# Agent attention and maxout FFN: queries turned on TensorE, keys still turned by DMA

## The chip, the core and the metric

The kernel runs on one core of a Trainium2 chip. The metric is the device time of one execution in microseconds; the median of three runs is taken. The engines named below are TensorE (PE for its matmuls, PEld for its weight loads), VectorE (DVE), ScalarE (ACT), GpSimd (POOL) and SyncE (SP), which here only issues DMAs.

## What is computed

```python
B, N, C = (4, 12544, 128); n_agents = 49; d_ff = 768
def _attn_ref(q, k, v, agents):
    scale = 1.0 / np.sqrt(q.shape[-1])
    def sm(a, b):                       # softmax over the last axis
        s = scale * (a @ b.transpose(0, 2, 1))
        s = s - s.max(-1, keepdims=True)
        e = np.exp(s)
        return e / (e.sum(-1, keepdims=True) + 1e-09)
    agent_v = sm(agents, k) @ v
    return sm(q, agents) @ agent_v
def _moe_ref(x, w1, w2, w3, w_out):     # x: the attention's rows
    h = np.maximum(np.maximum(x @ w1, x @ w2), x @ w3)
    return h @ w_out
```

The 49 agents first read all 12,544 keys and values of a batch; then every query attends to the 49 agents, and each resulting row passes the FFN. Inputs and output are float32; the kernel works in bfloat16.

## The kernel before

A batch has 98 tiles of 128 rows, taken in 13 groups: twelve of 8 tiles (1,024 rows) and a last one of 2. There are 52 key groups (`k_group`) and 52 query groups (`q_group`). A key group is loaded, cast to bf16 on POOL, turned by a DMA transpose on SP (line 159), multiplied with the agents (`scores`, line 166), put through exp on ACT, and multiplied with the values and with ones (`values`, lines 178 and 180); DVE adds the sums into `Eacc` (`accumulate`, line 189). After a batch's last key group `k_tail` folds agent values and FFN weights into one matrix `G` (line 220). A query group is loaded, cast on POOL (line 249), turned by a DMA transpose on SP (line 253), multiplied with the agents (`scores`, line 259), put through exp (line 264), and multiplied with slices of `G`.

The maxout is written with two relus. For each of six slices f of the hidden width, `first(f)` on TensorE fills a `uv` tile, `relu_first(f)` on ACT takes its relu to `a_sb` (line 301), `second(f)` fills another `uv` tile, and `max_second(f)` on DVE takes the maximum into `r` (line 312). For f = 5 both steps are relus on ACT (lines 298 and 310) and `first(5)` and `second(5)` share one tile. Each `first` or `second` is two matmuls of line 287, on two halves of the rows. `out_linear` (line 317) and `out_hidden` (line 326) sum the result in an `o` tile, and `out_scale` on DVE (line 333) divides by the sum of the exponentials, which `recips` prepared from `sums` (line 273).

[...] three `uv` tiles of two banks, one `o` tile and one `m` tile. The single `m` buffer is handed from user to user: key scores with values and query sums, then query scores, then key scores again. An operation that takes a new `m` tile waits until the readers of the old one are done.

The order of all work is written out by hand. Each step is entered with a key, a float that counts slots; the steps are sorted by it, equal keys in the order of entry, and each engine executes its own in that order. Query group i has `key` 6i, so one group takes six slots. The key group one batch and one group ahead has the same key. In the six slots of a period TensorE's order is therefore, by key within the period: `out_linear(0)` 0.1, `out_hidden` 0.3, key `scores` 0.65, `second(1)` 1.0, `first(2)` 1.05, `out_hidden` 1.3, `second(2)` 2.0, `sums` and `first(3)` 2.05, `out_hidden` and key `values` 2.3, `second(3)` 3.0, `first(4)` 3.05, `second(4)` 4.0, `first(5)` 4.05, `out_linear(1)` 4.06, query `scores` of the next group 4.25, `out_hidden` 4.3, `second(5)` 5.0, `first(0)` of the next group 5.05, `out_hidden` 5.3, then `second(0)` and `first(1)` of the next group. DVE's order is `out_scale(1)` 0.1, three `max_second`, `recips` 2.6, `accumulate` 2.75, `out_scale(0)` 2.9, and two more `max_second` at 3.5 and 4.5.

Of the kernel before, what the change touches and what calls it, by code (L numbers as in the profile page):

```python
# [10 lines left out]
BF16 = mybir.dt.bfloat16  # L11
# [5 lines left out]
def kernel(  # L17
# [18 lines left out]
    nc = tc.nc  # L36
# [4 lines left out]
    P = 128  # L41
    NF = Dff // P
    H = 64
    GT = 8
# [10 lines left out]
    work = ctx.enter_context(tc.tile_pool(name="work", bufs=2))  # L55
# [8 lines left out]
    def m_tile(dtype=FP32):  # L64
        return psum.tile([P, 512 if dtype == FP32 else 1024], dtype, tag="m", bufs=1, name="m_ps")
# [3 lines left out]
    def at(key, fn):  # L69
        ops.append((key, len(ops), fn))  # L70


    ident = const.tile([P, P], BF16, name="ident")
# [3 lines left out]
    agT = const.tile([P, B, H], BF16, name="agT")  # L77
# [9 lines left out]
    for i, w in enumerate((moe_w1, moe_w2, moe_w3)):  # L87
        t = const.tile([P, Dff], FP32, name=f"wst{i}")
# [143 lines left out]
    def q_group(b, g):  # L232
        n, t0 = sizes[g], starts[g] * P
        nh = n // 2
        T = nh * P
        pairs = [range(0, min(2, nh)), range(2, nh)]
        key = 6.0 * (NG * b + g)
        d = {}
# [10 lines left out]
            nc.gpsimd.tensor_copy(out=d["qb"][:, :n, :], in_=d["q"][:, :n, :])  # L249

        def transposes():
            d["qT"] = work.tile([P, GT, P], BF16, tag="qT", bufs=3, name="qT")
            nc.sync.dma_start_transpose(out=d["qT"][:, :n, :],
                                        in_=d["qb"][:, :n, :].rearrange("p j c -> p (j c)"))

        def scores():
            t = d["s"] = m_tile()
            for h in range(2):
                nc.tensor.matmul(t[h * H:(h + 1) * H, :T], agT[:, b, :], d["qT"][:, h:n:2, :],  # L259
                                 start=True, stop=True, skip_group_check=True)  # L260

        def exps():
# [79 lines left out]

        at(key - 24, load)
        at(key - 14, cast)
        at(key - 10.2, transposes)
        at(key - 1.75, scores)
        at(key - 1.3, exps)
        at(key + 2.05, sums)
# [21 lines left out]
    for b in range(B):  # L370
        for g in range(NG):
            k_group(b, g)
            q_group(b, g)
# [34 lines left out]
```

## Time and profile before

| | |
|---|---|
| median of 3 runs | 603.34 us (602.93 to 603.52) |
| profiled execution | 602.93 us, its span 601.1 us |
| loads and stores on SP | 512 KB each; 48 of each of k, v, q and out, and 4 small ones of each |
| DMA transposes on SP | 52 of kT, median 5.2 us to landing; 52 of qT, median 4.5 us |
| HBM traffic | 78.74 MB read, 25.69 MB written |

The span runs from the first to the last instruction of the profiled execution. A line of the groups gives busy time, the mean duration of one, and the idle time of the engine just before, with what ended it. Three stages are to be kept apart. Until about 70 us only key groups of the first batch run. From there to about 450 us query groups of one batch and key groups of the next run together. After that only queries of the last batch are left.

### The profile page before, as it was taken

What the parts mean: (1) busy time and instruction counts of PE and PEld (TensorE: products, weight loads), DVE (VectorE), ACT (ScalarE), POOL (GpSimd) and SP (SyncE); (2) the same over time, 40 slices, a digit from 0 to 9 for tenths busy, and PEclk for the clock granted to TensorE, in tenths of its full rate; (3) what the DMA queues carried; (4) which work ended last, traced back from release to release, by engine and by line L of the source; (5) the groups of instructions that cost most, each with busy time, mean ns of one, the idle gap of its engine ahead of it and who ended that gap; (6) DMA issues with size and microseconds to landing.
All of it is one profiled execution on the core that took longest, in us unless ns stands there. A gap on an engine that the chain in (4) does not pass through costs nothing.

```text
span 601.1 us, 13157 instructions
## 1 busy us (share of the span) xinstructions
PE 471.4 (78%) x5320; PEld 285.2 (47%) x5320; DVE 383.8 (64%) x499; ACT 412.5 (69%) x493; POOL 140.3 (23%) x149
## 2 busy tenths in 40 slices
PE   0343588898987889888887878889896898889886
PEld 0333245555553545555553545555553444545454
DVE  1200267878786556878776568787875667766774
ACT  2542378787875667787875678878784577777773
POOL 1223543233142232323142232322000101010000
PEclk9999999999998969999997989999996889988999
DMA  8999999999898797989986899995732625533222
GB/s 325 370 340 343 341 275 303 270 294 219 252 239 225 222 277 198 270 269 202 255 261 196 216 284 224 284 257 159 181 110 53 189 77 147 145 119 101 67 75 81
DMA packets 135112, 130.99 MB, mean 218 GB/s; under 512 B 107079, under 2 KB 110091, under 8 KB 135051
## 3 DMA queue, kind: packets, MB, share of 16 engines
q1 hardware_dynamic: 133632, 128.48, 76.7%
q10 hardware_dynamic: 1419, 1.67, 0.8%
q8 instruction: 41, 0.67, 0.5%
q14 instruction: 20, 0.16, 0.1%
HBM read 78.74 MB, written 25.69 MB: 174 GB/s over the span
## 4 chain that ended last, share of the span: by engine, by line
PE 49%; ACT 18%; DVE 15%; DMA 9%; issue 6%; SPq 1%; POOL 1%; ACTq 0%; POOLq 0%; DVEq 0%
PE uv_ps L287 20%; PE o_ps L326 18%; ACT a_sb L301 14%; DVE r L312 12%; DMA kT<-k_bf 6%; PE o_ps L317 4%; PE m_ps L259 3%; DVE o_sb L333 3%; ACT r L310 2%; DMA qT<-q_bf 1%; PE m_ps L178 1%; PE m_ps L180 1%; DMA wst<-in_moe_w_dram 1%; PE m_ps L220 1%; POOL k_bf L150 1%
## 5 line engine op out<-in xcount | busy, mean ns | idle before, releaser
L312 DVE TENSOR_TENSOR r<-uv_ps,a_sb 128x1024 bf16<-128x1024 f32 (+1 forms) x260 | 295.0, 1158 | 40.7 <-ACT a_sb L301 27.7
L301 ACT ACTIVATE a_sb<-uv_ps 128x1024 bf16<-128x1024 f32 (+1 forms) x260 | 248.3, 975 | 71.7 <-PE uv_ps L287 69.9
L287 PE MATMUL uv_ps<-e_q,G 49*128 49x512 bf16 (+1 forms) x1248 | 211.8, 391 | 55.0 <-ACT a_sb L301 43.6
L326 PE MATMUL o_ps<-wo_bf,r 128*128 128x128 bf16 x2352 | 184.1, 227 | 0.0
L326 PEld LDWEIGHTS <-r 128*128 128x128 bf16 x2352 | 144.4, 101 | 52.0 <-issue 49.2
L287 PEld LDWEIGHTS <-G 49*128 49x128 bf16 x1248 | 65.5, 95 | 131.8 <-issue 93.4
L333 DVE TENSOR_TENSOR o_sb<-o_ps,recips 128x512 f32<-128x512 f32 (+1 forms) x100 | 67.0, 670 | 95.1 <-PE o_ps L326 95.1
L249 POOL CAST q_bf<-q_st 128x1024 bf16<-128x1024 f32 (+1 forms) x52 | 51.7, 994 | 154.3 <-DMA qT<-q_bf 150.0
L155 POOL CAST v_bf<-v_st 128x1024 bf16<-128x1024 f32 (+1 forms) x39 | 38.7, 993 | 207.4 <-PE m_ps L180 187.2
L298 ACT ACTIVATE uv_ps<-uv_ps 128x1024 f32<-128x1024 f32 (+1 forms) x52 | 49.9, 959 | 28.5 <-DVE r L312 16.0
L310 ACT ACTIVATE r<-uv_ps 128x1024 bf16<-128x1024 f32 (+1 forms) x52 | 50.7, 975 | 21.5 <-PE uv_ps L287 21.4
L150 POOL CAST k_bf<-k_st 128x1024 bf16<-128x1024 f32 (+1 forms) x52 | 51.9, 998 | 55.5 <-DMA kT<-k_bf 46.4
L317 PE MATMUL o_ps<-G,e_q 128*128 128x256 bf16 x196 | 40.3, 287 | 12.7 <-DVE o_sb L333 12.5
L166 PE MATMUL m_ps<-agT,kT 128*128 128x49 bf16 x392 | 20.9, 196 | 25.7 <-DMA kT<-k_bf 24.4
L178 PE MATMUL m_ps<-e_k,v_bf 128*128 128x49 bf16 x392 | 30.8, 195 | 8.7 <-ACT e_k L171 8.7
L171 ACT ACTIVATE e_k<-m_ps 128x392 bf16<-128x392 f32 (+1 forms) x52 | 25.0, 480 | 16.1 <-PE m_ps L166 15.8
L189 DVE TENSOR_TENSOR Eacc<-m_ps,Eacc 128x98 f32<-128x98 f32 x48 | 10.6, 221 | 35.7 <-PE m_ps L180 35.7
L264 ACT ACTIVATE e_q<-m_ps 128x512 bf16<-128x512 f32 (+1 forms) x52 | 29.5, 568 | 3.7 <-PE m_ps L259 3.6
L317 PEld LDWEIGHTS <-e_q 128*128 128x128 bf16 x196 | 15.0, 98 | 35.1 <-issue 34.5
L180 PE MATMUL m_ps<-e_k,ones 128*128 128x49 bf16 x392 | 30.9, 194 | 0.0
L180 PEld LDWEIGHTS <-ones 128*128 128x128 bf16 x392 | 26.0, 103 | 10.0 <-issue 10.0
L166 PEld LDWEIGHTS <-kT 128*128 128x128 bf16 x392 | 17.3, 104 | 28.3 <-DMA kT<-k_bf 25.7
(43 smaller groups left out, 137.3 us busy)
## 6 DMA issues: line engine op xcount, KB each, us to landing
k_st<-in_k_dram SPq DMA_DIRECT2D x48, 512.0 KB, 5.4
v_st<-in_v_dram SPq DMA_DIRECT2D x48, 512.0 KB, 6.2
q_st<-in_q_dram SPq DMA_DIRECT2D x48, 512.0 KB, 4.2
out_dram<-o_sb SPq DMA_DIRECT2D x48, 512.0 KB, 2.9
wst<-in_moe_w_dram ACTq DMA_DIRECT2D x3, 384.0 KB, 7.8
kT<-k_bf SPq DMA_TRANSPOSE x52, 5.2
qT<-q_bf SPq DMA_TRANSPOSE x52, 4.5
k_st<-in_k_dram SPq DMA_DIRECT2D x4, 128.0 KB, 4.6
```

The costliest lines, as they stand in the source:

```text
L150: nc.gpsimd.tensor_copy(out=d["kb"][:, :n, :], in_=d["k"][:, :n, :])
L155: nc.gpsimd.tensor_copy(out=d["vb"][:, :n, :], in_=d["v"][:, :n, :])
L180: nc.tensor.matmul(t[:, c + A:c + 2 * A], ones, e, start=False, stop=True, skip_group_check=True)
L249: nc.gpsimd.tensor_copy(out=d["qb"][:, :n, :], in_=d["q"][:, :n, :])
L287: nc.tensor.matmul(t[:, h, :T], G[b][h * H:h * H + A, col + f * P:col + (f + 1) * P], d["e"][h * H:h * H + A, :T], start=start, stop=True, ...
L298: nc.scalar.activation(u, u, AF.Relu)
L301: nc.scalar.activation(a_sb[f][:, :, :T], u, AF.Relu)
L310: nc.scalar.activation(r[:, :, :T], u, AF.Relu)
L312: nc.vector.tensor_tensor(out=r[:, :, :T], in0=u, in1=a_sb[f][:, :, :T], op=ALU.max)
L317: nc.tensor.matmul(t[:, i * 2 * C:(i + 1) * 2 * C], d["e"][:, jj * P:(jj + 1) * P], G[b][:, C1O:C1O + 2 * C], start=(i == 0), stop=False, ...
L326: nc.tensor.matmul(t[:, c:c + C], r_sb[f][:, h, jj * P:(jj + 1) * P], wo_bf[:, f, :], start=False, stop=(f == NF - 1), skip_group_check=True)
L333: nc.vector.tensor_tensor(out=d["out"][:, j:j + m, :], in0=d["o", o][:, :m * C].rearrange("p (j c) -> p j c", c=C), in1=d["r"][:, j:j + m] ...
```

## The change

Only the query side changes. The DMA transpose of line 253 goes. In its place the eight 128x128 blocks of a group are turned by eight TensorE transposes (matmuls against an identity) into an `m` tile of bf16, and a new step `evacuate` copies that tile on DVE to `qT` in SBUF. The blocks of even and odd tiles are put apart on the way, so that `scores` reads two contiguous halves. The transposes are entered at key - 3.0 (before: key - 10.2) and the copy at key - 2.6. `qT` has two buffers in place of three. The keys' side keeps its DMA transposes.

```diff
         def transposes():
-            d["qT"] = work.tile([P, GT, P], BF16, tag="qT", bufs=3, name="qT")
-            nc.sync.dma_start_transpose(out=d["qT"][:, :n, :],
-                                        in_=d["qb"][:, :n, :].rearrange("p j c -> p (j c)"))
+            t = d["qT_ps"] = m_tile(BF16)
+            for j in range(n):
+                jj, h = divmod(j, 2)
+                i = h * nh + jj
+                nc.tensor.transpose(t[:, i * P:(i + 1) * P], d["qb"][:, j, :], ident)
+
+        def evacuate():
+            d["qT"] = work.tile([P, GT * P], BF16, tag="qT", name="qT")
+            nc.vector.tensor_copy(out=d["qT"][:, :n * P], in_=d["qT_ps"][:, :n * P])
 
         def scores():
             t = d["s"] = m_tile()
             for h in range(2):
-                nc.tensor.matmul(t[h * H:(h + 1) * H, :T], agT[:, b, :], d["qT"][:, h:n:2, :],
+                nc.tensor.matmul(t[h * H:(h + 1) * H, :T], agT[:, b, :], d["qT"][:, h * T:(h + 1) * T],
                                  start=True, stop=True, skip_group_check=True)
...
-        at(key - 10.2, transposes)
+        at(key - 3.0, transposes)
+        at(key - 2.6, evacuate)
```

## Prediction

> **What bounds the kernel now.** First the page. TensorE is the busiest engine, but no engine is full, and its clock is mostly, not always, granted.
>
> ```profile
> span 601.1 us, 13157 instructions
> PE 471.4 (78%) x5320; PEld 285.2 (47%) x5320; DVE 383.8 (64%) x499; ACT 412.5 (69%) x493; POOL 140.3 (23%) x149
> PEclk9999999999998969999997989999996889988999
> ```
>
> Next the list of waits from 76 us to the end, TensorE alone. Its first two lines:
>
> ```profile
> PE uv_ps L287 <- ACT a_sb L301: 43.6, 52, 0.9
> PE o_ps L317 <- DVE o_sb L333: 12.5, 47, 0.8
> ```
>
> No line of that list names a DMA. Over the whole span the page has 24.4 us of TensorE waiting for kT, all in the first 76 us, where keys run alone; TensorE waited 0.9 us for qT, once.
>
> Then the chain of waits in a stretch of steady state, one period of 9.73 us (relu to relu, 128.47 to 138.21):
>
> ```profile
> 135.00 1.24 DVE r L312
> 136.23 0.04 issue
> 136.27 0.39 PE uv_ps L287 x2
> 136.67 0.55 PE o_ps L326 x8
> ...
> 137.57 0.03 PE m_ps L178
> 137.60 0.03 PE m_ps L180
> 137.63 0.56 PE uv_ps L287 x4
> 138.18 0.02 issue
> 138.21 1.03 ACT a_sb L301
> 139.24 0.04 issue
> 139.28 0.39 PE uv_ps L287 x2
> ```
>
> The period is a closed loop: `max_second(1)`, `first(3)`, `out_hidden`, the key values, `second(3)` and `first(4)` (the x4), `relu_first(4)` on ACT, `first(5)`, and by way of TensorE, ACT and DVE back. There is no slack on it. What is put between the values and `first(4)` lengthens every period.
>
> The timeline of the same place, by engine, shows what lies beside it:
>
> ```profile
> 137.67 0.21 DVE L279 RECIPROCAL recips<-m_ps 128x8 f32<-128x8 f32 x1 [0.25 <-PE m_ps L180]
> 137.79 0.21 DVE L189 TENSOR_TENSOR Eacc<-m_ps,Eacc 128x98 f32<-128x98 f32 x1
> 137.92 0.68 DVE L333 TENSOR_TENSOR o_sb<-o_ps,recips 128x512 f32<-128x512 f32 x1
> 138.52 2.35 DVE L312 TENSOR_TENSOR r<-uv_ps,a_sb 128x1024 bf16<-128x1024 f32 x2
> 142.53 0.69 DVE L333 TENSOR_TENSOR o_sb<-o_ps,recips 128x512 f32<-128x512 f32 x1 [1.67 <-PE o_ps L326]
> ```
>
> The `m` tile is free of its readers only when `accumulate` ends, at 138.00.
>
> **What the Trainium skill says.** "TensorE: Matmul & The Clock Gate", Part 4, says that a TensorE transpose goes to PSUM and needs a copy after it, and that in transpose mode it "doesn't count as PE-busy the same way". On the time this trace disagrees with nothing: the six transposes of the weights (line 123) lasted 314 ns at the median and started within 0.5 us (24.5 to 25.0), as did six plain matmuls of the same shape (line 127, 26.0 to 26.5). On the counting no run here shows anything. Part 1 of that page says that the clock is halved or given back by the activity of windows of about 3.4 us; the trace agrees, and shows how near the edge this kernel runs (below). "VectorE: DVE Perf Modes", tier table, allows a copy out of PSUM at most twice the base rate. "Perfetto Trace Analysis", Matmuls, advises rotating PSUM banks so that evacuation overlaps; here the transposes have the one `m` bank.
>
> **The change part by part.** *Removed:* 52 DMA transposes and their issues on SP. As no wait of TensorE after 76 us names a DMA, and the first qT is issued at 61.99 us, behind the chain's last kT (53.41), I count this at nothing. POOL's 150.0 us of waiting for qT turn into waits of the same cast for the transposes of two groups before, as `qb` has two buffers. Those end at that group's key - 3, one slot before the cast at key - 14 of the later group is due. The casts of k and v and then SP's kT, queued behind it, have 14 slots, some 23 us, until the key scores; kT lands in 5.2 us. That is the cover; without it a late kT would stop TensorE.
>
> *Eight transposes, in TensorE's order.* Their key ties with `second(3)`, which was entered earlier; so they stand after `second(3)` and before `first(4)`. They wait for `accumulate`: 138.00 + 0.05 = 138.05. Eight 128x128 matmuls cost 0.55 us in the chain until the next thing starts, changeover included. `first(4)` started at 137.79 (timeline); now 138.60: **+0.81 us**, 0.26 of waiting and 0.55 of work. Waiting behind them are `first(4)`, and through it ACT's relu, `first(5)` and the rest of the loop.
>
> *The copy on DVE.* Nearest row: w1T, 768 bf16 out of PSUM, 557 ns; four copies of 49 took 179 ns. So 0.53 ns an element, 1,024 take 0.69 us. It runs from about 138.7 to 139.4, between `out_scale(0)` and `max_second(3)`, which start 0.8 late. Who needs them: the query scores, before at 139.93, now 140.74, need the copy (1.3 us to spare); `first(0)`, about 141.3 before and 142.1 now, needs the tile of `max_second(3)`, which ends about 140.6. So it costs nothing. Its upper bound, at the base rate, is near the 1.2 us of a 1,024-wide row of line 312: still within the 1.3. DVE's idle 1.67 us before `out_scale(1)` takes it up.
>
> *The groups.* In batches 0 to 2 the 33 full groups g = 1 to 11: 33 x 0.81 = 26.7. Their three groups of two tiles, work 0.21 in place of 0.55: 3 x 0.47 = 1.4. The first groups of batches 1 to 3 stand behind `k_tail`, whose last copy ended at 191.42 in the first case, and run at half clock, where twelve of line 326 took 1.46 us: about 3 x 1.1 = 3.3. Batch 3 has no `accumulate`: the transposes wait for `recips` (end 576.28), 576.33 + 0.55 = 576.88 in place of `first(4)` at 576.22, 0.66 each: 11 x 0.66 + 0.3 = 7.6. The very first group: `Eacc`'s copy ends at 69.54, transposes at half clock and their latency 1.1, copy 0.7; scores at 71.4 in place of 70.12: 1.3. Two more groups at the cold start pay 0.4 extra each: 0.8. Sum **41.1 us**; 602.93 + 41.1 = 644.0 for the profiled execution, and 644 against the median 603.34, 0.4 us above it.
>
> **The rivals.**
>
> *The clock falls.* The windows view, over stretches that end where the clock record changed or could have:
>
> ```profile
> 524.40:527.80 3.40, 2.46 (x25) 1.20 (x24) 3.34 (x5) 2.60 (x3) 1.04 (x1) 1.00 0.93 248
> 527.80:531.20 3.40, 3.40 (x20) 1.67 (x21) 1.34 (x2) 1.61 (x2) 0.00 (x0) 0.50 0.00 0
> 575.60:579.00 3.40, 2.48 (x23) 1.01 (x21) 3.40 (x5) 2.61 (x3) 0.00 (x0) 1.00 0.01 2
> 128.40:131.80 3.40, 2.50 (x26) 1.19 (x21) 2.73 (x3) 2.54 (x3) 1.60 (x3) 1.00 1.22 196
> ```
>
> After the first comes half clock, after the third and fourth not: the lowest windows are already at the edge, 2.46 of 3.40 us busy against 2.48. The change puts a wait into just that part of the period, where `first(5)` already waits 0.90 us. If the transposes count as work, I take the windows to stay about where they are. If not, the low window loses 0.45 us more. Each halving in batch 3 made its two exp-to-exp intervals together 1.4 us longer (9.79 + 10.52 against 2 x 9.43). A low stretch of about 1.9 us, met by windows 3.4 us apart, is hit in 0.56 of the periods: 48 x 0.56 x 1.4 = 38 us on top, **682**. For it: the skill's sentence. Against it: a transpose moves as many columns at the same pace.
>
> *The transposes are slower than matmuls when the clock is full.* The trace has them only in the cold start, 107 ns apart. If they kept to that pace, 8 x 0.05 more per group, 20 us in all: **664**.
>
> *VectorE becomes the bound.* Should the copy or `max_second(3)` miss its margin of 1.3 us, its 0.69 enters the loop as well: 48 x 0.69 = 33, **677**. Against it: DVE has 23% idle in a period.
>
> *The other side.* The loop has 0.90 us of idle TensorE before `first(5)` in every period. If the transposes ran there, 0.55 would vanish in it, and as work they would lift the low windows and save the two halvings in batch 3, 2.8 us: **600.5**. It decides where `first(4)` is delayed by less than about 0.1 us. Against it: the order of equal keys.
>
> **How the numbers follow.** The sum holds: 0.50. The clock falls: 0.36. VectorE: 0.06. Slow transposes: 0.04. The other side: 0.04. The likeliest is 644, its own range 634 to 655 (0.26 of waiting and changeover either way, 48 times 0.2). The range goes to 702, to take in most of the clock's case, 660 to 720. Faster by over 0.2%, about what a measurement of this kernel can tell from no change: 0.03; within it 0.02; slower 0.95.
>
> **What would show it.** Right: the exp of the queries comes every 10.55 us in place of 9.73 in steady state, `first(4)` starts some 0.6 us after `accumulate` ends, PE waits a little for `Eacc`, and the copies last about 0.69 us. The clock's case: half clock in many slices of the steady state. Wrong: an interval under 9.9, `first(5)`'s wait shrunk, or TensorE waiting for kT.

## The result, and the profile after

| | before | after |
|---|---|---|
| median, and its runs | 603.43 us (602.93 to 606.06, 4 runs) | 645.76 us (645.34 to 646.15, 4 runs) |
| profiled execution, span | 602.93 us, 601.1 us | 645.34 us, 643.6 us |

The ratio is 1.0692, 95% interval 1.066 to 1.0724. The change is slower, by 42.5 us between the two spans. The forecast was 644. Here and below a median is that of all runs, while a ratio leaves out runs more than 1.5% above the fastest of their kernel.

The lines of the changed kernel have moved: transposes 256, copy 260, query scores 265, query exp 270, `recips` 285, `first` and `second` 293, `relu_first` 307 (304 for f = 5), `max_second` 318 (316), `out_linear` 323, `out_hidden` 332, `out_scale` 339. The key side has its old lines. First the page after: totals, clock, and the two new groups (line, operation, count | busy, mean ns | idle before it, and what ended most of that).

```profile
PE 506.0 (79%) x5712; PEld 309.5 (48%) x5712; DVE 417.2 (65%) x551; ACT 412.1 (64%) x493; POOL 138.3 (21%) x149
PEclk9999999999998979999996779999997959999999
...
L260 DVE COPY qT<-m_ps 128x1024 bf16<-128x1024 bf16 (+1 forms) x52 | 34.3, 660 | 12.4 <-PE m_ps L256 11.1
L256 PE MATMUL m_ps<-ident,q_bf 128*128 128x128 bf16 x392 | 32.2, 227 | 8.9 <-DVE Eacc L189 6.0
```

The shares are nearly those of before, and the clock has its dips only at the batch changes. The two dips that batch 3 had before are gone. So 42.5 us went without an engine becoming busier in its share: a sign of a longer loop, not of a fuller engine. The waits of TensorE from 80 us on say the same (us in total, times, longest):

```profile
PE uv_ps L293 <- ACT a_sb L307: 43.9, 52, 0.9
PE o_ps L323 <- DVE o_sb L339: 12.5, 47, 0.8
PE m_ps L256 <- DVE Eacc L189: 6.0, 31, 0.2
```

The first two are the old ones, unchanged (43.6 and 12.5 before). The third is the new one. TensorE waits as long for ACT as before, and does 0.5 us more ahead of it. The chain of waits in one period (start, length, what):

```profile
145.03 0.39 PE uv_ps L293 x2
145.42 0.55 PE o_ps L332 x8
...
146.42 0.21 DVE recips L285
146.62 0.14 DVE Eacc L189
146.76 0.14 issue
146.90 0.61 PE m_ps L256 x8
147.50 0.34 PE uv_ps L293 x2
...
147.87 1.03 ACT a_sb L307
148.90 0.04 issue
148.94 0.39 PE uv_ps L293 x2
```

Where `second(3)` and `first(4)` stood together in one x4 before, the chain now leaves TensorE for `recips` and `accumulate` on DVE, comes back with 0.14 us of "issue", spends 0.6 on the transposes, and only then reaches `first(4)` (the x2 at 147.50), ACT's relu and `first(5)` (148.94). The timelines of TensorE and DVE there show where the loop was cut open, and what lies beside it:

```profile
146.90 0.61 PE L256 MATMUL m_ps<-ident,q_bf 128*128 128x128 bf16 x8 [0.19 <-DVE Eacc L189]
147.44 0.61 PE L293 MATMUL uv_ps<-e_q,G 49*128 49x512 bf16 x4
148.94 0.39 PE L293 MATMUL uv_ps<-e_q,G 49*128 49x512 bf16 x2 [0.90 <-ACT a_sb L307]
...
149.59 0.41 PE L265 MATMUL m_ps<-qT,agT 128*64 128x512 bf16 x2
```

```profile
146.54 0.21 DVE L189 TENSOR_TENSOR Eacc<-m_ps,Eacc 128x98 f32<-128x98 f32 x1
146.67 0.68 DVE L339 TENSOR_TENSOR o_sb<-o_ps,recips 128x512 f32<-128x512 f32 x1
147.54 0.69 DVE L260 COPY qT<-m_ps 128x1024 bf16<-128x1024 bf16 x1 [0.19 <-PE m_ps L256]
```

The 0.68 of `out_scale` lies beside the wait and the transposes. TensorE idles before the transposes and again, 0.90 us, before `first(5)`. The copy ends at 147.54 + 0.69 = 148.23, and the query scores that need it start at 149.59, 1.36 later. In the whole span they waited for it 0.8 us in total.

Starts of the query exps in the two traces, from one group to the next, give the loss by place:

| | before, us | after, us | difference | in the forecast's sum |
|---|---|---|---|---|
| first exp | 70.80 | 72.36 | +1.56 | +1.3 |
| batch 0, first and second interval | 9.95, 11.26 | 11.21, 13.54 | +1.26, +2.28 | +1.2 each |
| steady interval, batches 0 to 2 | 9.73 | 10.65 | +0.92 | +0.81 |
| steady interval, batch 3 | 9.43 | 10.08 | +0.65 | +0.66 |
| batch 0 (first exp to that of batch 1) | 132.3 | 145.4 | +13.1 | +11.3 |
| batch 1 | 135.5 | 146.0 | +10.6 | +10.5 |
| batch 2 | 133.0 | 142.9 | +9.9 | +10.5 |
| batch 3, to its last exp | 116.9 | 124.3 | +7.4 | +7.6 |

1.56 + 13.1 + 10.6 + 9.9 + 7.4 = 42.5 us, each rounded by itself. From the last exp to the end the two take 12.6 and 12.5.

### The profile page after: what moved, and what is told of

Same layout as the page of the kernel before. It is cut to its first block, busy times and chain, and to the rows that moved or that the text cites. A ratio compares the mean times of both kernels' runs of the same rounds, so it can differ in the third digit from the quotient of the medians.

```text
span 643.6 us, 13846 instructions
## 1 busy us (share of the span) xinstructions
PE 506.0 (79%) x5712; PEld 309.5 (48%) x5712; DVE 417.2 (65%) x551; ACT 412.1 (64%) x493; POOL 138.3 (21%) x149
## 3 DMA queue, kind: packets, MB, share of 16 engines
q1 hardware_dynamic: 81792, 115.63, 56.3%
## 4 chain that ended last, share of the span: by engine, by line
PE 48%; DVE 17%; ACT 17%; issue 8%; DMA 7%; POOL 1%; SPq 1%; DVEq 0%; ACTq 0%; POOLq 0%
PE uv_ps L293 16%; PE o_ps L332 16%; ACT a_sb L307 13%; DVE r L318 11%; DMA kT<-k_bf 6%; PE m_ps L256 5%; PE o_ps L323 4%; PE m_ps L265 3%; DVE o_sb L339 2%; ACT r L316 2%; DVE recips L285 2%; PE m_ps L220 1%; PE m_ps L178 1%; PE m_ps L180 1%; DMA k_st<-in_k_dram 1%
## 5 line engine op out<-in xcount | busy, mean ns | idle before, releaser
L293 PE MATMUL uv_ps<-e_q,G 49*128 49x512 bf16 (+1 forms) x1248 | 219.1, 393 | 54.5 <-ACT a_sb L307 44.5
L323 PE MATMUL o_ps<-G,e_q 128*128 128x256 bf16 x196 | 40.0, 286 | 12.5 <-DVE o_sb L339 12.5
L260 DVE COPY qT<-m_ps 128x1024 bf16<-128x1024 bf16 (+1 forms) x52 | 34.3, 660 | 12.4 <-PE m_ps L256 11.1
L256 PE MATMUL m_ps<-ident,q_bf 128*128 128x128 bf16 x392 | 32.2, 227 | 8.9 <-DVE Eacc L189 6.0
L256 PEld LDWEIGHTS <-q_bf 128*128 128x128 bf16 x392 | 24.8, 100 | 22.5 <-issue 21.3
L189 DVE TENSOR_TENSOR Eacc<-m_ps,Eacc 128x98 f32<-128x98 f32 x48 | 10.6, 221 | 35.7 <-PE m_ps L180 35.7
```

Source lines behind the costliest of these rows:

```text
L256: nc.tensor.transpose(t[:, i * P:(i + 1) * P], d["qb"][:, j, :], ident)
L293: nc.tensor.matmul(t[:, h, :T], G[b][h * H:h * H + A, col + f * P:col + (f + 1) * P], d["e"][h * H:h * H + A, :T], start=start, stop=True, ...
L323: nc.tensor.matmul(t[:, i * 2 * C:(i + 1) * 2 * C], d["e"][:, jj * P:(jj + 1) * P], G[b][:, C1O:C1O + 2 * C], start=(i == 0), stop=False, ...
```

## The experiments

Ratios are against the kernel before, run beside each. All kernels start from the changed one.

**Eight transposes, one place later.** The same work, behind `first(4)` in place of ahead of it.

```diff
-        at(key - 3.0, transposes)
+        at(key - 2.94, transposes)
```

> The eight transposes are entered at key - 2.94 in place of key - 3.0, so that they stand behind first(4) and before second(4); nothing else changes. Theory A (place): first(4) and relu_first(4) run at their old time, the transposes and their wait for accumulate fall into the 0.90 us in which TensorE waits for relu_first(4) before first(5), and the period goes back from 10.65 to 9.73 us in steady state and from 10.08 to about 9.43 in the last batch: 605 to 609 us. Rival B (amount): eight more matmuls on TensorE and a copy on VectorE cost their time wherever they stand: 640 us or more. Rival C (clock): transposes do not count as TensorE's activity, so that the low windows fall below the edge and half clock comes into the steady state: over 625 us.

Measured: 602.75 us, ratio 0.9953 (0.9933 to 0.9973), intervals 9.73 and 9.43 as before the change. Timeline of TensorE and its waits from 80 us on:

```profile
139.52 0.60 PE L293 MATMUL uv_ps<-e_q,G 49*128 49x512 bf16 x4
140.10 0.61 PE L256 MATMUL m_ps<-ident,q_bf 128*128 128x128 bf16 x8
140.64 0.39 PE L293 MATMUL uv_ps<-e_q,G 49*128 49x512 bf16 x2
141.24 0.39 PE L293 MATMUL uv_ps<-e_q,G 49*128 49x512 bf16 x2 [0.21 <-ACT a_sb L307]
```

```profile
PE uv_ps L293 <- ACT a_sb L307: 10.6, 46, 0.6
```

`second(3)` and `first(4)` are one x4 again. The eight transposes start without a wait and use up idle time that was there anyway: the wait for the relu falls from 0.90 to 0.21 us, in total from 43.9 to 10.6. So the same eight transposes and the same copy cost 42 us in one place and nothing in the other; the two buffers of `qT` and the new layout that `scores` reads are in this kernel as well. The place is the cause; the amount of work alone is not. The total lies 2 us below the forecast of 605 to 609; where that comes from was not traced.

**The same transposes one place earlier.** Ahead of `second(3)` as well.

```diff
-        at(key - 3.0, transposes)
+        at(key - 3.05, transposes)
```

> The transposes are entered at key - 3.05 in place of key - 3.0, so that they stand before second(3). Theory A: they start at the same moment, as accumulate sets it, but second(3), 0.22 us, which filled most of the wait, now comes after them and before first(4): 0.22 more in each of 48 periods, steady period 10.87 and 655 to 658 us. Rival (only the matmuls' work counts): 645 to 647 us as before.

Measured: 660.7 us, ratio 1.0923 (1.0832 to 1.1014), intervals 10.86 and 10.30. Its chain of waits:

```profile
146.88 0.14 DVE Eacc L189
147.01 0.14 issue
147.15 0.61 PE m_ps L256 x8
147.76 0.56 PE uv_ps L293 x4
...
148.34 1.03 ACT a_sb L307
```

Now the x4 stands behind the transposes, 0.56 in place of 0.34 us: +0.22, and the steady interval grew by 0.21. The total came out above its forecast of 655 to 658: in the profiled execution, the slower of the two runs, 2.0 us more pass after the last exp (14.5 in place of 12.5), and some 6 around the batch changes. With the first experiment this gives a scale for these kernels: what was put ahead of `first(4)` counted in full, and what stood behind it counted not at all as long as it fitted into the 0.90 us gap.

**The transposes twice**, each into the same place of the tile.

```diff
-                nc.tensor.transpose(t[:, i * P:(i + 1) * P], d["qb"][:, j, :], ident)
+                for _ in range(2):
+                    nc.tensor.transpose(t[:, i * P:(i + 1) * P], d["qb"][:, j, :], ident)
```

> Every transpose is issued twice, to the same place; the order stays. Theory A: eight more at 0.055 us stand on the loop, 0.44 us in each of 48 periods and a little in the small groups and at half clock: 667 to 671 us, with the steady state at full clock. Rival B (the wait for the m tile is the cost, not the work): under 652 us. Rival C (transposes do not count as activity): half clock in many periods and over 685 us.

Measured: 668.07 us, ratio 1.1039 (1.0976 to 1.1103); intervals 11.09 (+0.44) and 10.53 (+0.45). Eight more transposes cost 0.44 us, so 0.055 each, and the total lies in the forecast range. The steady state kept full clock. That speaks against slow transposes, against the wait for the `m` tile as the whole cost, and against a fall of the clock.

**The copy twice, and four times.**

```diff
-            nc.vector.tensor_copy(out=d["qT"][:, :n * P], in_=d["qT_ps"][:, :n * P])
+            for _ in range(2):
+                nc.vector.tensor_copy(out=d["qT"][:, :n * P], in_=d["qT_ps"][:, :n * P])
```

The second kernel has `range(4)`.

> The copy of qT out of PSUM is made twice. Theory A: VectorE has 1.4 us between the end of the copy and the query scores that need it (148.23 to 149.66 in the changed kernel's trace), one more copy takes 0.6: no change, within 2 us of the changed kernel. Rival (VectorE is in the loop): 0.6 us in each of 48 periods, 29 us: about 675 us.

> The copy is made four times: 1.8 us more on VectorE against the 1.4 us of room. Theory A: the query scores start some 0.4 to 0.5 us late and are on the loop: 660 to 672 us. Rival (VectorE is in the loop): 3 x 0.6 us in each of 48 periods, 88 us: about 734 us. Rival (the copy has more room than this, as the scores can wait): no change.

Measured: twice, 651.9 us (650.99 to 652.81), ratio 1.0772 (1.0711 to 1.0833); four times, 718.54 us, ratio 1.1873 (1.1808 to 1.1939). Both totals miss their forecasts, 6 us above the changed kernel where at most 2 were expected, and 718.54 us where 660 to 672 were. Of the first, the steady intervals are as expected: 10.65 and 10.08, within 0.01. The extra us lie outside them, about 1.0 before the first exp, 2.0 in the third interval (12.67 against 10.65), and the rest at batch changes. In the third interval half clock lasted longer: there twelve matmuls of `out_hidden` took 1.39 us, in the changed kernel 0.78. So a copy more is free in the loop, and not at the start.

Four times shows where the margin ends. Timeline of TensorE and of DVE:

```profile
147.09 0.39 PE L324 MATMUL o_ps<-G,e_q 128*128 128x256 bf16 x2
148.29 0.41 PE L266 MATMUL m_ps<-qT,agT 128*64 128x512 bf16 x2 [0.80 <-DVE qT L261]
```

```profile
145.37 2.87 DVE L261 COPY qT<-m_ps 128x1024 bf16<-128x1024 bf16 x4 [0.20 <-PE m_ps L256]
```

The copies now end 2.87 - 0.69 = 2.18 later in the loop than one; the margin was 1.36, so 0.82 should show, and the scores waited 0.80 (the forecast had 0.6 for each further copy; they took 0.73). But many intervals are 12.6 to 13.0, not 10.65 + 0.80 = 11.45. The windows say why (busy us and instructions of PE, PEld, DVE, ACT and POOL, then clock, DMA share, GB/s):

```profile
157.00:160.40 3.40, 1.70 (x16) 0.78 (x13) 3.30 (x5) 2.25 (x3) 2.92 (x3) 1.00 0.17 59
160.40:163.80 3.40, 3.40 (x28) 2.08 (x27) 1.67 (x3) 2.25 (x3) 0.00 (x0) 0.50 0.00 0
```

TensorE was busy 1.70 of 3.40 us, and in the next window the clock was halved. In batches 0 to 2, 16 of the 27 intervals from the third to the eleventh of a batch were of this longer kind, and there the wait of 0.80 us brought 1.2 to 1.5 us more. The expectation had put the clock at nothing.

**The first group earlier**, on top of the first experiment. Its transposes need no `m` tile if they use a `uv` tile, idle at that time.

```diff
-            t = d["qT_ps"] = m_tile(BF16)
+            t = d["qT_ps"] = uv_bf16() if (b, g) == (0, 0) else m_tile(BF16)
...
-        at(key - 2.94, transposes)
-        at(key - 2.6, evacuate)
+        early = 8.5 if (b, g) == (0, 0) else 0.0
+        at(key - 2.94 - early, transposes)
+        at(key - 2.6 - early, evacuate)
```

> As the run with the transposes behind first(4), and the very first query group alone is turned some 8.5 slots earlier, through a uv bank that is idle at the start, while TensorE waits for the keys. Theory A: the first query scores come at about 70 us in place of 71.7, and the time is 1.5 to 2 us below that run, a ratio to before of 0.990 to 0.994. Rival: the start is set by the keys' chain alone, and the ratio stays at that run's 0.995.

Measured: 600.54 us, ratio 0.9919 (0.9898 to 0.9941). The first exp starts at 70.72 us in place of 72.47 in the first experiment: without the single `m` tile the first group's transposes are off the path. In the kernel before, the chain to the first exp ran through the first group's DMA transpose, 8.09 us, and that exp started at 70.80. So even there its removal brought almost nothing: in this run the scores wait for the keys' last `Eacc` copy, which ends at 70.00.

**The DMA transposes of the queries kept as well**, into a tile that nothing reads, on top of the first experiment.

```diff
+        def dma_too():
+            x = work.tile([P, GT, P], BF16, tag="qTx", bufs=3, name="qTx")
+            nc.sync.dma_start_transpose(out=x[:, :n, :],
+                                        in_=d["qb"][:, :n, :].rearrange("p j c -> p (j c)"))
+
+        at(key - 10.2, dma_too)
```

> As the run with the transposes behind first(4), but the 52 DMA transposes of the queries are issued as before as well, into a tile that nothing reads. Theory A: the DMA transposes were worth nothing in time, as no wait of TensorE after 76 us names a DMA: periods of 9.73 us and a ratio to before within 0.002 of that run's 0.9953. Rival: it is the relief of the DMA engines and of SP's queue that brought that run below the kernel before: a ratio of 1.00 or more.

Measured: 602.4 us, ratio 0.9977 (0.995 to 1.0005); intervals 9.74 and 9.43. In steady state the 52 DMA transposes are worth nothing, which is what the forecast had put for their removal. In the total the two ratios differ by 0.0024, where at most 0.002 was expected, with intervals that overlap, and this one reaches 1.0005; a few tenths of a per cent, at the start or the batch changes, are neither shown nor excluded.

**The keys of batch 0 turned on TensorE too**, on top of the fifth. In the chain of the changed kernel kT is the largest piece of the start, 54% of the first 72 us; here batch 0's keys take the `uv` tiles as well.

```diff
+        def turn():
+            t = d["kT_ps"] = uv_bf16()
+            for j in range(n):
+                nc.tensor.transpose(t[:, j * P:(j + 1) * P], d["kb"][:, j, :], ident)
+
+        def evacuate():
+            d["kT"] = work.tile([P, GT, P], BF16, tag="kT", bufs=3, name="kT")
+            nc.vector.tensor_copy(out=d["kT"][:, :n, :].rearrange("p j c -> p (j c)"),
+                                  in_=d["kT_ps"][:, :n * P])
...
-        at(key - 8.2, transposes)
+        if b == 0:
+            at(key - 3.9, turn)
+            at(key - 3.6, evacuate)
+        else:
+            at(key - 8.2, transposes)
```

> As the run with the first group early, and the keys of batch 0 alone, which run before there is other work, are turned on TensorE through the idle uv banks as well; the keys of batches 1 to 3 keep their DMA transposes. Theory A: in the first 60 us a key group takes 3.45 us, set by the cast, the DMA transpose and two buffers; without the DMA the loads set about 3.1 us, and the last kT's 6.5 us to landing shrinks to about 2: the first query scores come at 60 to 66 us in place of 70, ratio to before 0.976 to 0.988. Rival (the loads already set the start): ratio within 0.003 of the run with the first group early.

Measured: 592.93 us, ratio 0.9777 (0.9707 to 0.9848, three runs), the fastest of all; whether it is more than 2% faster than before stays open. The chain of waits up to the first query exp, first in the changed kernel, then in this one:

```profile
53.64 6.61 DMA kT<-k_bf
...
69.89 1.03 PE m_ps L256 x8
...
70.94 0.70 DVE qT L260
...
71.69 0.65 PE m_ps L265 x2
...
72.36 0.61 ACT e_q L270
```

```profile
23.59 9.14 DMA v_st<-in_v_dram
...
33.90 7.34 DMA v_st<-in_v_dram
...
61.40 0.65 PE m_ps L282 x2
...
62.07 0.61 ACT e_q L287
```

The first exp comes 10.3 us earlier than in the changed kernel. The kT transfers have left the chain, and the loads of v stand in it, with half of its time up to the first exp. The last of them ends at 41.2 us; from there on the chain runs through TensorE, ACT, DVE and POOL.

## Why the prediction was right

**Sign, size and place** were right. The first experiment shows the cause by itself: one key moved, nothing else, and the loss is gone. Term by term:

- *The wait before the transposes was the mis-sized term.* The forecast had 0.05 us from the end of `accumulate` to the first transpose, taken from how soon `first(3)` restarts after `max_second`. Measured: 146.76 to 146.90, 0.14 us. The transposes themselves took 0.54 (146.90 to 147.44 in the timeline), as put (0.55). Before, `first(4)` had started 0.21 ahead of `accumulate`'s end; so 0.21 + 0.14 + 0.54 = 0.89 of the 0.92 a period are placed, where the forecast had 0.81. Behind `first(4)` the wait is gone. The trace shows what stands in the longer wait:

```profile
L256 PEldq EVENT_SEMAPHORE  x35: 51/51/51, 79.2 to 478.8; - x35
```

  In 35 groups of batches 0 to 2 TensorE's weight-load queue has a semaphore instruction of 51 ns of its own between the end of the DVE step and the first transpose; the first weights are loaded behind it (146.87), and the first transpose follows 0.03 us later. Where it is missing, the forecast's 0.05 holds, as in batch 3, where the first weights were loaded at 587.40, ahead of the end of `recips`:

```profile
587.36 0.21 DVE recips L285
587.56 0.04 issue
587.61 0.61 PE m_ps L256 x8
```

  Why the one wait gets an instruction of its own and the other does not, the runs do not show.
- *Batch 3*, where the transposes wait for `recips` and no longer for `accumulate`: +0.65 against 0.66.
- *The copy*: 691 ns for 1,024 elements against 0.69, and free in the loop. Its margin was 1.36 us, where the forecast had 1.3; the fourfold copy bears it out (2.18 - 0.80 = 1.38).
- *The first group*: +1.56 against 1.3. The fifth experiment takes just this off and gains 1.75 us at the first exp.
- *Cold start*: the two intervals cost 3.54 together where 2.4 stood. The second alone grew by 2.28, as half clock lasted longer: eight matmuls of `out_hidden` still took 0.97 us at 91.03 in the changed kernel, while before they took 0.55 from 87.99 on.
- *Batch changes*: the sum has 1.1 a batch. In each kernel other windows lose the clock there, 12.73 and 11.02 us before against 12.02 and 10.64 after in the same intervals of batch 1, so the steady loss of about 0.1 more per period is paid back in part. That the totals agree within 1.4 us (42.5 against 41.1) is in part luck: steady periods and cold start cost more than put, and the batch changes less.
- *The DMA transposes' removal at nothing*: right in steady state. No wait of TensorE after 80 us names a DMA in the changed kernel, though the share of queue q1 fell from 76.7% to 56.3%.

**The rivals.** The fall of the clock had 0.36, for a sentence of the Trainium skill ("TensorE: Matmul & The Clock Gate", Part 4), that a transpose does not count as activity. The runs disagree. (The trace lists the transposes as MATMUL with `ident`; whether the chip's transpose mode was on, it does not say.) Here is a window of 3.4 us of the changed kernel and the next one, all instructions, and then the transposes of the first alone:

```profile
278.60:282.00 3.40, 2.31 (x27) 1.05 (x23) 3.00 (x6) 1.48 (x3) 1.98 (x3) 1.00 0.94 367
282.00:285.40 3.40, 3.16 (x36) 2.00 (x36) 1.58 (x2) 3.14 (x4) 1.03 (x2) 1.00 0.20 80
```

```profile
278.60:282.00 3.40, 0.61 (x8) 0.46 (x8) 1.00 0.94 367
```

The same of the kernel with the transposes doubled:

```profile
267.33:270.74 3.41, 2.31 (x26) 1.32 (x24) 2.77 (x6) 1.11 (x2) 1.88 (x2) 1.00 1.00 387
270.74:274.16 3.42, 3.33 (x36) 1.90 (x35) 1.68 (x2) 2.86 (x4) 1.13 (x2) 1.00 0.11 40
```

```profile
267.33:270.74 3.41, 1.05 (x16) 0.91 (x16) 1.00 1.00 387
```

Without the transposes 2.31 - 0.61 = 1.70 us and 2.31 - 1.05 = 1.26 us of work are left. The clock stayed full after both. It was lost after the window of 1.70 without a transpose in the kernel with four copies (above), and after 2.46 in the kernel before. Busy time alone does not order the windows, as it counts overlaps and fill loosely: the kernel before kept the clock after 2.39 (241.08 to 244.49). So the prediction's edge between 2.46 and 2.48 was none. I therefore also counted how much of each window matmuls fill if 128 columns take 55 ns, the step from one transpose of a row to the next, with overlaps counted once. From 70 us on, the kernel before lost the clock after windows filled to at most 0.47 and kept it from 0.49 on; with the transposes counted, the changed kernel lost it up to 0.42 and kept it from 0.47 on, and the doubled one up to 0.42 and from 0.49 on. Uncounted, 43 windows of the doubled kernel that kept it would be filled to less than 0.45, the lowest to 0.26. So the transposes are counted. The edge is not sharp: the kernel with four copies kept the clock after 0.42 and lost it after 0.45.

*Slow transposes* fall with the doubled kernel, 0.055 us each. *VectorE* falls by the margin of 1.36 us. *The other side* was described rightly, with the 0.90 us gap and its edge at `first(4)`, and does not happen at this key; 0.06 of a slot further on it does, 602.75 us (604.29 for the kernel before beside it) against the 600.5 priced (603.34).

## What to carry to other kernels

Where a closed chain sets the period, ask of added work first which instruction of the chain it stands ahead of, and only then how long it lasts. Here the same work cost 9.2% ahead of `second(3)`, 6.9% between it and `first(4)`, where equal keys and the order of entry had put it, and nothing 0.06 of a slot later. Put such work into the gap where its engine waits anyway, directly behind the instruction that feeds that wait. Then look at the cold start by itself: there transposes on TensorE can win, as those of batch 0's keys did, because the transfers that they replaced were on its path.

## What the runs showed of the hardware that was not expected

- Transposes kept the clock up like other matmuls: it stayed full after windows of 2.31 us with 1.70 and 1.26 without them, and was lost after 1.70 us of other work.
- A further 0.80 us of idle TensorE in a period, 11.45 us long with it, brought half clock in about every other period, 1.2 to 1.5 us on top. This kernel, near the edge, paid for a small wait more than its length.
- From the end of a DVE instruction to the first transpose that waited for it passed 0.14 us where a semaphore instruction of 51 ns and then the weight load came in between, and 0.05 where the weights had been loaded ahead of the wait.
